# Batch 1's values and mix results take the path of later batches, batch 2's loads move, odd mixes move by 0.4 slots

## The chip, the cores and the metric

The kernel runs on one core of a Trainium2 chip. The metric is the device time of one execution in microseconds (us), lower is better; times before are the median of three runs. A profile is of one execution, and its span is a little shorter than that execution's time.

## What is computed

Eight batches of pooled attention, followed by a token mix and a channel MLP with affine scales and residuals. Keys and values are averaged over groups of 8 tokens, so 576 tokens give 72 pooled ones.

```python
# q, k, v: (8 batches, 8 heads, 576 tokens, 64)
k_p = k.reshape(B, H, 72, 8, D).mean(axis=3)
v_p = v.reshape(B, H, 72, 8, D).mean(axis=3)
attn = softmax(q @ k_p.T / 8)
x = (attn @ v_p) in the layout (B, 576, 512)
a1 = alpha1 * x + beta1
u = x + lam * einsum('ts,bsd->btd', w_tok, a1)
a2 = alpha2 * u + beta2
out = u + lam * (maximum(a2 @ w_ch1, 0) @ w_ch2)     # 512 -> 2048 -> 512
```

All inputs and the output are fp32; the matmuls take bf16 or fp16.

## The kernel before

The tokens of all batches are cut into 36 chunks of 128 rows. A batch has four chunks of 128 tokens and 64 tokens left over; the 64 of an even batch and of the odd one after it share a chunk. The list `chunks` puts them in this order: (0,0) to (0,3), (1,0) to (1,3), then (0,4), the shared one, then (2,0) and so on. Four chunks in this order make a block, of 512 rows, for the MLP: nine blocks, n = 0 to 8. Block 1 is exactly the four chunks (1,0) to (1,3); block 3 is (2,3), (3,0), (3,1), (3,2).

While TensorE works through the MLP of block n, the attention and token mix of batch n+1 are put between its matmuls. The order is written out by hand: for each block a list `todo` of pairs (slot, action) is filled and sorted by slot, and the actions are then issued in that order; every engine works through its own part of it strictly in order. A slot is about one group of four 512-wide matmuls. Slots 0 to 15 are `mlp_A(n, j)` (first MLP matmul, L604, ReLU on ScalarE, L609). Slots 16 to 31 are `mlp_B(n, m, part)` (second matmul, L638), four parts for each row group m; with the last part VectorE scales the sum by lam (L644), adds it to u (L645), and SP issues the store of the output (L647). Where slots are equal, what was put in the list first comes first. Batch 0 and the constants come before block 0, in a straight hand-written sequence.

One batch's attention has these steps:

- `load_k` (L91, SP) loads fp32 keys, two tiles of four heads; `sum_k` on POOL adds them pairwise (L160, L162); `att_K` pools on TensorE (L405, L411), and VectorE copies the result to `kp` (L417). With `behind` given, `load_k`, `load_v` and `load_rem` first write a tiny memset with that engine, so that the load is not issued before the engine's place in the order.
- The queries come in bf16 by a casting DMA from POOL (L77). `att_F` transposes them, with TensorE for batches 0 and 1 and by a transposing DMA from SP (L363) from batch 2 on. `cast_rem`, `att_Frem` and `rem_qT` do the same for the 64 remaining tokens.
- The values. Batches 0 and 1 load them in fp16 by a casting DMA from POOL (`load_v16`, L106 and L111), and `first_V` pools them with six matmuls for each half of the heads (L431, L433), with two copies by VectorE (L436). From batch 2 on `load_v` loads fp32 values by SP (L137), 72 partitions with 8 tokens each, one tile for each half of the heads, and `att_V` pools one pair of heads with three VectorE additions (L443 twice, L445). The tag `v_u` has two buffers for both kinds of tile.
- `att_S4` computes the scores of four heads (L475, L482) from `kp` and the queries, ScalarE the exponentials, `att_AV` the weighted values (L519, L523) and their division by the sums (L525, L527), `att_X` the scaled input `xs` of the mix (L534, L538).
- `mix_T(b, c)` is the token mix of chunk c (L567); VectorE adds the residual (L571) and writes a bf16 copy `u_bf` (L574; four buffers).
- `mix_uT` turns `u_bf` into columns of `u_fm`, the input of `mlp_A`. For batches 0 and 1 TensorE transposes (L588) and ScalarE copies (L590); for later batches and for the shared chunk (0,4) SP issues a transposing DMA (L583). One matmul of `mlp_A(n, 0)` reads the columns of all four chunks of its block.

SP's queue, in order, holds key, value and remainder loads, the transposing DMAs and the output stores; a store waits in it for VectorE's L645. POOL's queue holds the casting DMAs of queries and weights (`load_w1`, `load_w2`) between POOL's arithmetic.

The list of block 0 for batch 1 (`first`), as far as it matters: `att_K(1,0)` and `att_K(1,1)` at slots 6.4 and 9.4, `att_S4(1,0)` and `att_S4(1,1)` at 9.0 and 13.6, `bias_row(1)` on VectorE at 4.5, `first_V` at 11.0 and 12.2. The mixes of every batch are at 21.0 + 1.3c.

Of the kernel before, what the change touches and what calls it, by code (L numbers as in the profile page):

```python
# [23 lines left out]
def kernel(  # L24
# [18 lines left out]
    nc = tc.nc  # L43
# [27 lines left out]
    def rows(src, b, u):  # L71
        return src[b, 4 * u:4 * u + 4, 0:512, :].rearrange("h (p c) d -> p h (c d)", c=4)
# [13 lines left out]
    def load_k(b, u, behind=None):  # L86

        raw = work.tile([P, 4, 4, D], FP, tag="k_raw", bufs=2, name="k_raw")
        if behind is not None:
            behind.memset(raw[:, 0, 0, 0:1], 0.0)  # L90
        nc.sync.dma_start(out=raw.rearrange("p h c d -> p h (c d)"), in_=rows(k, b, u))  # L91
        st1[b]["raw"][u] = raw

    def load_v16(b, parts=(0, 1, 2)):

        if 0 in parts:
            t = work.tile([P, 6, H, D], F16, tag="v_u", bufs=2, name="v16")
            main, rest = t[:, 0:4].rearrange("p c h d -> p (c h d)"), t[0:32, 4:6]
            main = main.rearrange("p (h c d) -> p h c d", h=H, c=4)
            rest = rest.rearrange("p c h d -> p (c h d)").rearrange(  # L100
                "p (h c d) -> p h c d", h=H, c=2)
            st1[b]["v"] = main, rest
        main, rest = st1[b]["v"]
        for part in parts:
            if part == 1:
                nc.gpsimd.dma_start(  # L106
                    out=rest.rearrange("p h c d -> p h (c d)"),
                    in_=v[b, :, 512:576, :].rearrange("h (p c) d -> p h (c d)", c=2))
            else:
                u = part // 2  # L110
                nc.gpsimd.dma_start(  # L111
                    out=main[:, 4 * u:4 * u + 4].rearrange("p h c d -> p h (c d)"),
                    in_=rows(v, b, u))
# [188 lines left out]
    def setup_rowsum(tcx):  # L302

        trc = P if tcx < 4 else REM
        cols = slice(P * tcx, P * tcx + trc)
        ps = gp("ps_rs")
        for sc in range(5):
            nc.tensor.matmul(out=ps[:, 0:trc], lhsT=ones_bf if sc < 4 else ones_lo,
                             rhs=wtT[:, sc, cols], start=(sc == 0), stop=(sc == 4))
        nc.scalar.copy(out=wtT[64:65, 4, cols], in_=ps[64:65, 0:trc])  # L310
# [128 lines left out]
    def att_V(b, hp):  # L439

        t = st1[b]["v"][hp // 2][:, 2 * (hp % 2):2 * (hp % 2) + 2]
        for n in (4, 2):
            nc.vector.tensor_tensor(out=t[:, :, 0:n], in0=t[:, :, 0:n], in1=t[:, :, n:2 * n],  # L443
                                    op=ALU.add)
        nc.vector.tensor_tensor(out=vp1_pool[hp][:, :, 0:64], in0=t[:, :, 0], in1=t[:, :, 1],  # L445
                                op=ALU.add)
# [129 lines left out]
    def mix_uT(key):  # L576
        s = st2[key]
        i = where[key]
        blk, at = i // 4, i % 4
        if blk not in u_fm:  # L580
            u_fm[blk] = work.tile([P, 4, 512], BF, tag="u_fm", bufs=3, name="u_fm")
        if key[0] > 1 or key == (0, 4):
            nc.sync.dma_start_transpose(out=u_fm[blk][:, :, 128 * at:128 * at + 128],  # L583
                                        in_=s["u_bf"])
            return
        ps_uT = gp("ps_uT").bitcast(BF)
        for cc in range(4):
            nc.tensor.transpose(out=ps_uT[0:P, 128 * cc:128 * cc + 128],  # L588
                                in_=s["u_bf"][:, 128 * cc:128 * cc + 128], identity=identity_bf)
        nc.scalar.copy(out=u_fm[blk][:, :, 128 * at:128 * at + 128],  # L590
                       in_=ps_uT[:, 0:512].rearrange("p (c t) -> p c t", t=128))
# [115 lines left out]
    att_AV(0, 7)  # L707
    for u in range(2):
        load_k(1, u, nc.vector)
    setup_rowsum(0)  # L710
    setup_wtok(2, nc.scalar.copy)
    setup_rowsum(1)
# [2 lines left out]
    setup_rowsum(2)  # L715
    keep_warm(1)
    load_w1(3)
    load_v16(1, (0, 1))
    setup_rowsum(3)
    mix_T(0, 0, nc.gpsimd)  # L720
    mix_T(0, 1, nc.gpsimd)
    load_v16(1, (2,))
    for g in range(3):
        load_w2(g)
    setup_bias(0)
# [16 lines left out]
    def attention(b):  # L742


        first = b == 1
        todo = []
        if first:
            for hp in range(4):
                todo.append((2.6 + 0.9 * hp, lambda hp=hp: att_F(b, hp)))
            todo.append((3.5, lambda: cast_rem(b, nc.gpsimd)))  # L750
            todo.append((3.65, lambda: load_w2(3)))
            todo.append((7.4, lambda: att_Frem(b, nc.scalar.copy)))
        if b < B - 1:
            at = 27.0 if first else 10.0
            todo.append((at, lambda: att_F(b + 1, 0)))
            todo.append((at + 0.1, lambda: att_F(b + 1, 2)))
            at = 28.0 if first else 25.5
            todo.append((at - 1.0, lambda: cast_rem(b + 1, nc.gpsimd)))
            todo.append((at, lambda: att_Frem(b + 1)))
        for u in range(2):  # L760
            todo.append((3.6 + 0.1 * u if first else -0.9 + 1.2 * u,
                         lambda u=u: sum_k(b, u, nc.gpsimd)))
            todo.append((6.4 + 3.0 * u if first else 4.1 + 2.0 * u,
                         lambda u=u: att_K(b, u, nc.vector.tensor_copy)))
            if first:
                todo.append((11.0 + 1.2 * u, lambda u=u: first_V(b, u)))
        for u in range(2):
            at = (9.0 if first else 6.3, 13.6)[u]
            todo.append((at, lambda u=u: att_S4(b, u)))
            for k, dt in enumerate((0.1, 0.1, 0.1, 0.7, 1.7, 1.75) if u else (0.1, 0.1, 0.1, 1.1, 2.1, 3.1)):  # L770
                todo.append((at + dt, lambda u=u, k=k: st1[b]["exp", u](k)))
            for i, dt in enumerate((2.9, 3.4, 4.6, 5.1) if u else (5.7, 6.2, 2.9, 3.4)):
                h = 4 * u + i
                todo.append((at + dt, lambda h=h: att_AV(b, h)))
                if i % 2:
                    todo.append((at + dt + 0.1, lambda h=h: att_X(b, h - 1, h + 1)))
        if not first:
            for hp in range(4):
                todo.append((0.2 + 2.0 * hp, lambda hp=hp: att_V(b, hp)))
        for c in range(5):  # L780
            at = 21.0 + 1.3 * c
            if c < 4 or b % 2:
                todo.append((at, lambda c=c: mix_T(b, c)))
                key = (b, c) if c < 4 else (b - 1, 4)
                if first and c in (2, 3):
                    at += 1.3 * c - 2.0
                elif first and c < 2:
                    at += 1.0
                todo.append((at + 1.8, lambda key=key: mix_uT(key)))
        return todo  # L790

    for n in range(NBLK):
        todo = []
        for j in range(0 if n else 4, NJ):
            todo.append((j, lambda j=j: mlp_A(n, j)))
        for m in range(4):
            for part in range(4):
                at = 16 + 4 * m + part
                todo.append((at, lambda m=m, part=part: mlp_B(n, m, part)))
        if n == 0:  # L800
            todo.append((4.5, lambda: bias_row(1)))
            todo.append((6.2, lambda: setup_rowsum(4)))
            todo.append((8.3, setup_wtok_odd))
            for g in range(2, 4):
                todo.append((4 * g - 0.8, lambda g=g: setup_bias(g)))
        if n == NBLK - 1:
            for g in range(4):
                todo.append((2.0 + 3.0 * g, lambda g=g: scale_w2(g)))
        b = n + 1
        if b < B:  # L810
            todo += attention(b)
            if b + 1 < B:
                new_batch(b + 1)
                gate = nc.vector if b == 1 else None
                for u in range(2):
                    at = 21.0 + 0.2 * u
                    todo.append((at, lambda b=b, u=u: load_k(b + 1, u, gate)))
                    at = (21.0 if b == 1 else 0.4) + 0.1 * u
                    todo.append((at, lambda b=b, u=u: load_q_bf(b + 1, u)))
                    at = 19.0 + 0.2 * u if b == 1 else 3.5 + 4.0 * u  # L820
                    todo.append((at, lambda b=b, u=u: load_v(b + 1, u, behind=gate)))
                todo.append((20.9, lambda b=b: load_rem(b + 1, behind=gate)))
        for _, do in sorted(todo, key=lambda x: x[0]):
            do()

# [29 lines left out]
```

The softmax here doesn't subtract the row's maximum and nothing guards it: scores larger than these inputs give would overflow.

## Time and profile before

| what | us |
|---|---|
| median of 3 runs | 352.65 (352.64 to 353.04) |
| the profiled execution | 353.1 |
| its span | 351.1 |
| TensorE busy | 337.8 |
| VectorE busy | 226.0 |
| first MLP matmul of block 0 (L604) | at 30.51 |
| first MLP matmul of block 1 | at 74.69 |
| first MLP matmul of block 2 | at 110.41 |
| first MLP matmul of block 3 | at 147.26 |

The profile gives, for each engine, its busy time and the idle time before an instruction with what ended it. PE is TensorE, PEld its weight loads, DVE VectorE, ACT ScalarE, POOL GpSimd, SP SyncE; SPq is SP's queue of DMA issues. Line numbers are those of the kernel before. Times of single instructions are from the start of the span. In timelines the columns are start, duration, engine, line, operation, output and inputs, count, and in brackets the idle time before with its releaser. Sizes of DMA packets are those written.

### The profile page before, as it was taken

How to read it: one execution, taken by the hardware profiler on the slowest of the kernel's cores; microseconds unless marked ns; L12 is line 12 of the kernel's file. 1: busy time of each engine (PE TensorE's matmuls, PEld its weight loads, DVE VectorE, ACT ScalarE, POOL GpSimd, SP SyncE). 2: the span in 40 equal slices, each digit the busy share in tenths (PEclk: the TensorE clock that was granted, in tenths of full speed). 3: DMA queues.
4: the chain of work that ended last, by engine and by line, in shares of the span. 5: the costliest groups of instructions: out<-in, count | busy, mean ns of one | idle time of the engine just before them, and what ended most of it. 6: DMA issues, size and time to landing. Idle time of an engine off the chain costs nothing.

```text
span 351.1 us, 5881 instructions
## 1 busy us (share of the span) xinstructions
PE 337.8 (96%) x2206; PEld 178.8 (51%) x2247; DVE 226.0 (64%) x476; ACT 150.6 (43%) x283; POOL 78.9 (22%) x93
## 2 busy tenths in 40 slices
PE   7989999999999999999999999999999999999995
PEld 2667654455544554455445544554455445545544
DVE  6564048788696769775967697948785883037511
ACT  4564972238502850087008800791069105703800
POOL 8578600072017000710071005300510000000000
PEclk9999999999999999999999999999999999999999
DMA  8999980898738942897189719991820032011012
GB/s 129 196 213 241 217 151 0 188 248 174 134 113 203 216 63 66 231 190 121 55 224 189 127 52 211 186 146 51 228 75 1 32 90 77 0 60 62 0 54 66
DMA packets 66045, 44.57 MB, mean 127 GB/s; under 512 B 32409, under 2 KB 57309, under 8 KB 66018
## 3 DMA queue, kind: packets, MB, share of 16 engines
q1 hardware_dynamic: 50486, 33.18, 39.4%
q0 software_dynamic: 15072, 10.76, 21.1%
q8 instruction: 17, 0.28, 0.3%
q10 hardware_dynamic: 460, 0.27, 0.3%
q14 instruction: 10, 0.08, 0.1%
HBM read 38.30 MB, written 9.44 MB: 136 GB/s over the span
## 4 chain that ended last, share of the span: by engine, by line
PE 85%; DVE 8%; ACT 3%; issue 2%; POOL 1%; POOLq 0%; DVEq 0%; ACTq 0%
PE ps_h L604 33%; PE ps_ch L638 30%; PE ps_tok L567 12%; DVE x_tm L527 2%; PE ps_s L475 2%; PE ps_av L519 2%; DVE xs L534 2%; DVE v_u L443 1%; PE ps_ch L627 1%; ACT wtT L299 1%; PE ps_kp L405 1%; DVE rec L525 1%; PE ps_sc L455 1%; DVE ps_ch L644 1%; PE ps_v L431 1%
## 5 line engine op out<-in xcount | busy, mean ns | idle before, releaser
L609 ACT ACTIVATE Hj<-ps_h,bias_cols 128x512 bf16<-128x512 f32 x144 | 98.4, 689 | 150.7 <-PE ps_h L604 149.2
L604 PE MATMUL ps_h<-u_fm,w 128*128 128x512 bf16 (+1 forms) x571 | 132.2, 374 | 2.0 <-ACT Hj L609 0.5
L638 PE MATMUL ps_ch<-w,Hj 128*128 128x512 bf16 x543 | 128.7, 379 | 1.1 <-issue 0.6
L604 PEld LDWEIGHTS <-w 128*128 128x128 bf16 x592 | 63.9, 114 | 52.4 <-issue 4.0
L638 PEld LDWEIGHTS <-Hj 128*128 128x128 bf16 x560 | 52.8, 98 | 60.9 <-issue 1.6
L567 PE MATMUL ps_tok<-xs,wtT 128*128 128x512 bf16 (+3 forms) x200 | 44.8, 380 | 1.9 <-DVE xs L534 1.8
L644 DVE TENSOR_TENSOR ps_ch<-lam_bc,ps_ch 128x512 f32<-128x512 f32 x32 | 22.2, 693 | 33.2 <-PE ps_ch L638 33.0
L145 POOL CAST rem_q<-rem_raw 128x256 bf16<-128x256 f32 x7 | 3.3, 475 | 151.6 <-DMA rem_raw<-in_q_dram 151.6
L571 DVE TENSOR_TENSOR u_sb<-x_tm,ps_tok 128x512 f32<-128x512 f32 (+1 forms) x40 | 27.3, 683 | 11.3 <-PE ps_tok L567 11.2
L527 DVE TENSOR_TENSOR x_tm<-ps_av,rec 128x320 f32<-128x320 f32 x64 | 31.5, 492 | 2.3
L645 DVE TENSOR_TENSOR u_sb<-u_sb,ps_ch 128x512 f32<-128x512 f32 x35 | 24.0, 687 | 13.7 <-PE ps_ch L638 12.5
L504 ACT ACTIVATE ET<-ps_s 72x512 f16<-72x512 f32 x56 | 32.3, 591 | 0.0
L525 DVE RECIPROCAL rec<-ps_av 128x5 f32<-128x5 f32 x64 | 12.2, 190 | 30.2 <-PE ps_av L523 30.0
L567 PEld LDWEIGHTS <-wtT 128*128 128x128 bf16 (+3 forms) x200 | 16.9, 100 | 23.6 <-DVE xs L534 3.4
L443 DVE TENSOR_TENSOR v_u<-v_u 72x512 f32<-72x512 f32 (+1 forms) x48 | 27.3, 570 | 0.8
L574 DVE TENSOR_TENSOR u_bf<-u_sb,al_bc 128x512 bf16<-128x512 f32 x34 | 25.8, 758 | 2.5 <-DMA u_fm<-u_bf 1.4
L160 POOL TENSOR_TENSOR k_raw<-k_raw 128x512 f32<-128x512 f32 x14 | 19.1, 1367 | 13.1 <-DMA k_raw<-in_k_dram 12.6
L534 DVE TENSOR_TENSOR xs<-x_tm,lamal_bc 128x512 bf16<-128x512 f32 x29 | 20.1, 692 | 1.0
L519 PEld LDWEIGHTS <-ET 72*128 72x128 f16 x256 | 14.1, 97 | 8.9 <-issue 0.4
L162 POOL TENSOR_TENSOR k_bf<-k_raw 128x512 bf16<-128x512 f32 x14 | 17.8, 1275 | 1.1
L519 PE MATMUL ps_av<-vp,ET 72*128 72x66 f16 x256 | 15.8, 193 | 0.2 <-issue 0.2
L417 DVE CAST kp<-ps_kp 128x288 bf16<-128x288 f32 x14 | 6.4, 456 | 12.9 <-PE ps_kp L411 12.3
(119 smaller groups left out, 228.0 us busy)
## 6 DMA issues: line engine op xcount, KB each, us to landing
out_dram<-u_sb SPq DMA_DIRECT2D x32, 256.0 KB
k_raw<-in_k_dram SPq DMA_DIRECT2D x14, 512.0 KB
v_u<-in_v_dram SPq DMA_DIRECT2D x12, 512.0 KB
q_bf<-in_q_dram POOLq DMA_DIRECT2D x16, 256.0 KB, 6.6
w<-in_moe_w_ch_dram POOLq DMA_DIRECT2D x8, 512.0 KB, 14.6
v<-in_v_dram POOLq DMA_DIRECT2D x4, 256.0 KB, 9.8
rem_raw<-in_q_dram SPq DMA_DIRECT2D x15, 64.0 KB
rem_raw<-in_k_dram SPq DMA_DIRECT2D x15, 64.0 KB
```

The source lines that it names most:

```text
L443: nc.vector.tensor_tensor(out=t[:, :, 0:n], in0=t[:, :, 0:n], in1=t[:, :, n:2 * n], op=ALU.add)
L504: nc.scalar.activation(out=o, in_=i, func=AF.Exp, bias=0.0, scale=0.125)
L519: nc.tensor.matmul(out=av[:, odd + c, :], lhsT=ET[:, m0:m0 + 128], rhs=vp1[:, hh, :])
L527: nc.vector.tensor_tensor(out=x[:, 1 - odd:6 - odd, dd:dd + D], in0=av[:, :, 0:64], in1=rec.unsqueeze(2).to_broadcast((P, 5, D)), op=ALU.mult)
L534: eng.tensor_tensor(out=xs[:, 0:4, cols], in0=x[:, 1:5, cols], in1=lamal_bc[:, cols].unsqueeze(1).to_broadcast((P, 4, D * (h1 - h0))), op= ...
L567: nc.tensor.matmul(out=ps_tok[p0:p1], lhsT=wtT[0:kk, at, P * c:P * c + p1 - p0], rhs=xs_pool[i][0:kk, sc, :], start=(sc == 0), stop=(sc == 4))
L571: nc.vector.tensor_tensor(out=s["u"][p0:p1, :], in0=x[p0:p1, 1 + c if c < 4 else 5 - 5 * i, :], in1=ps_tok[p0:p1, 0:DM], op=ALU.add)
L574: eng.tensor_tensor(out=s["u_bf"], in0=s["u"], in1=al2_bc, op=ALU.mult)
L604: nc.tensor.matmul(out=ps_h[:, t0:t1], lhsT=w1_of(cc, j), rhs=u_fm[n][:, cc, t0:t1], start=(cc == 0), stop=(cc == 3))
L609: nc.scalar.activation(out=t, in_=ps_h, func=AF.Relu, bias=bias_cols[:, j:j + 1], scale=1.0)
L638: nc.tensor.matmul(out=ps, lhsT=Hj[n, j][:, 128 * m:128 * m + 128], rhs=w2[j // 4][:, j % 4, :], start=(j == 0), stop=(j == NJ - 1))
L644: nc.vector.tensor_tensor(out=ps, in0=lam_bc, in1=ps, op=ALU.mult)
```

## The change

Batch 1 no longer takes batch 0's path. Its values are loaded as fp32 by SP, right after its keys, and pooled by `att_V` on VectorE at slots 4.0, 5.5, 7.0 and 8.5 of block 0; the two `load_v16` of batch 1 on POOL and its two `first_V` go. Its mix results go through the transposing DMA at the mix's slot + 1.8, as in later batches. The loads of batch 2 in block 0 move: values from slot 19.0 to 13.0, remainders from 20.9 to 16.9, keys and queries from 21.0 to 17.0. The mixes of all odd batches move from 21.0 + 1.3c to 21.4 + 1.3c, and their transposes with them.

```diff
@@ mix_uT
-        if key[0] > 1 or key == (0, 4):
+        if key[0] or key[1] == 4:
             nc.sync.dma_start_transpose(out=u_fm[blk][:, :, 128 * at:128 * at + 128],
                                         in_=s["u_bf"])
             return
@@ the sequence ahead of block 0
     for u in range(2):
         load_k(1, u, nc.vector)
+    for u in range(2):
+        load_v(1, u, behind=nc.vector)
     setup_rowsum(0)
...
     load_w1(3)
-    load_v16(1, (0, 1))
     setup_rowsum(3)
     mix_T(0, 0, nc.gpsimd)
     mix_T(0, 1, nc.gpsimd)
-    load_v16(1, (2,))
     for g in range(3):
         load_w2(g)
@@ attention(b)
-            if first:
-                todo.append((11.0 + 1.2 * u, lambda u=u: first_V(b, u)))
...
-        if not first:
-            for hp in range(4):
-                todo.append((0.2 + 2.0 * hp, lambda hp=hp: att_V(b, hp)))
+        for hp in range(4):
+            at = 4.0 + 1.5 * hp if first else 0.2 + 2.0 * hp
+            todo.append((at, lambda hp=hp: att_V(b, hp)))
         for c in range(5):
-            at = 21.0 + 1.3 * c
+            at = 21.0 + 0.4 * (b % 2) + 1.3 * c
             if c < 4 or b % 2:
                 todo.append((at, lambda c=c: mix_T(b, c)))
                 key = (b, c) if c < 4 else (b - 1, 4)
-                if first and c in (2, 3):
-                    at += 1.3 * c - 2.0
-                elif first and c < 2:
-                    at += 1.0
                 todo.append((at + 1.8, lambda key=key: mix_uT(key)))
@@ the loop over blocks, loads of batch b + 1
-                    at = 21.0 + 0.2 * u
+                    at = (17.0 if b == 1 else 21.0) + 0.2 * u
                     todo.append((at, lambda b=b, u=u: load_k(b + 1, u, gate)))
-                    at = (21.0 if b == 1 else 0.4) + 0.1 * u
+                    at = (17.0 if b == 1 else 0.4) + 0.1 * u
                     todo.append((at, lambda b=b, u=u: load_q_bf(b + 1, u)))
-                    at = 19.0 + 0.2 * u if b == 1 else 3.5 + 4.0 * u
+                    at = 13.0 + 0.2 * u if b == 1 else 3.5 + 4.0 * u
                     todo.append((at, lambda b=b, u=u: load_v(b + 1, u, behind=gate)))
-                todo.append((20.9, lambda b=b: load_rem(b + 1, behind=gate)))
+                todo.append((16.9 if b == 1 else 20.9, lambda b=b: load_rem(b + 1, behind=gate)))
```

## The prediction

> **What bounds the kernel now.** I read the page first: share of each engine, then the chain that ended last.
>
> ```profile
> PE 337.8 (96%) x2206; PEld 178.8 (51%) x2247; DVE 226.0 (64%) x476; ACT 150.6 (43%) x283; POOL 78.9 (22%) x93
> PE 85%; DVE 8%; ACT 3%; issue 2%; POOL 1%; POOLq 0%; DVEq 0%; ACTq 0%
> ```
>
> PE is busy nearly all the time and carries 85% of the chain, so PE work removed anywhere is worth its own length, and any new wait of PE is paid in full. Next come the timelines of PE and DVE around block 0, where nearly all of the change lies.
>
> ```profile
> 42.44 0.30 PE L475 MATMUL ps_s<-qT,kp 64*72 64x256 bf16 x2
> ...
> 45.67 0.60 PE L431 MATMUL ps_v<-v,pool_v 128*72 128x256 f16 x4
> 46.20 0.40 PE L433 MATMUL ps_v<-v,pool_vr 32*72 32x256 f16 x2
> 46.53 0.70 PE L349 MATMUL ps_bias<-b2c_bf,w 128*128 128x1 bf16 x16
> ...
> 74.69 4.48 PE L604 MATMUL ps_h<-u_fm,w 128*128 128x512 bf16 x20
> ```
>
> ```profile
> 38.83 0.46 DVE L417 CAST kp<-ps_kp 128x288 bf16<-128x288 f32 x1 [7.37 <-PE ps_kp L411]
> ...
> 73.13 0.69 DVE L645 TENSOR_TENSOR u_sb<-u_sb,ps_ch 128x512 f32<-128x512 f32 x1
> ...
> 112.02 1.14 DVE L443 TENSOR_TENSOR v_u<-v_u 72x512 f32<-72x512 f32 x2
> 113.19 0.29 DVE L445 TENSOR_TENSOR vp<-v_u 72x128 f16<-72x128 f32 x1
> ```
>
> PE reaches the first scores of batch 1 (L475) at 42.44; the keys that they need were copied by DVE at 38.83, after an idle DVE. Block 1's first matmuls start at 74.69, with no gap. A head pair's pooling on DVE (L443 twice, L445) takes 1.14 + 0.29 us. The third view is the DMA queues, asked for short windows (packets, MB, share); here 26 to 28 us, 30 to 32, 40 to 42, and 72 to 74. Queue 0 holds what POOL issues, queue 1 what SP issues.
>
> ```profile
> q0 software_dynamic: 308, 0.29, 86.8%
> q1 hardware_dynamic: 298, 0.14, 35.3%
> ...
> q1 hardware_dynamic: 239, 0.24, 44.9%
> q0 software_dynamic: 239, 0.24, 71.1%
> ...
> q0 software_dynamic: 125, 0.44, 109.6%
> ...
> q1 hardware_dynamic: 713, 0.77, 107.2%
> ```
>
> Two things are to be seen. Where both queues have work they send equal numbers of packets, even where the packets differ in size (298 of 0.5 KB against 308 of 0.9 KB). And queue 0's packets after 38 us, the w2 loads, are large: 0.44 MB in 125, some of which are tiny, so 4 KB each. The fourth view, POOL and SP:
>
> ```profile
> 33.62 1.27 POOL L160 TENSOR_TENSOR k_raw<-k_raw 128x512 f32<-128x512 f32 x1 [1.20 <-DMA k_raw<-in_k_dram]
> 37.94 1.26 POOL L160 TENSOR_TENSOR k_raw<-k_raw 128x512 f32<-128x512 f32 x1 [1.18 <-DMA k_raw<-in_k_dram]
> ```
>
> ```profile
> 23.14 1.24 SPq L91 DMA_DIRECT2D k_raw<-in_k_dram x2
> ...
> 74.31 3.32 SPq L363 DMA_TRANSPOSE qT<-q_bf x2
> 77.72 1.20 SPq L381 DMA_TRANSPOSE rem_qT<-rem_q x1
> 78.97 1.26 SPq L583 DMA_TRANSPOSE u_fm<-u_bf x1
> ```
>
> Batch 1's two key tiles, issued at 23.14, land only at 33.6 and 37.9: the DMA engines are the scarce thing from 18 to 50 us (the third to sixth slice of their row on the page read 9, 9, 9 and 8). The v of batch 1 will be queued behind these keys.
>
> **What the Trainium skill says.** "DMA: Bandwidth & Descriptors", section Queues, rings and completion order: each DMA engine goes round robin over the queues that have work, and changes only at packet boundaries. The windows above agree (239 against 239). It follows that a queue with small packets gets a small share of the bytes beside one with large ones. The same page, Issuing engines are not separate DMA queues: loads from POOL and SP share the same 16 engines, so moving v from one queue to the other frees no bandwidth. "TensorE: Matmul & The Clock Gate", section What's actually happening: after an idle window of about 3.4 us the PE clock halves, and comes back after about as long a busy one. The trace has a cold start that fits: four L431 matmuls took 0.95 us at 11.27 and 0.60 us at 45.67.
>
> **The change part by part.**
>
> *Removed from PE.* Two poolings of v: 45.67 to 46.53 and 48.19 to 49.06, 1.73 us. Sixteen transposes of mix results (L588): each four push the next work back 0.22 us (64.51 to 64.73), 0.88 us. Together 2.6 us of PE, all on the path. ACT loses four copies of 0.59 us and DVE four of 0.24; neither bounds there.
>
> *v of batch 1 by SP, pooled by DVE.* In DVE's order the poolings of head pairs 0 and 1 now stand ahead of the first kp copy (L417), and those of pairs 2 and 3 ahead of the second. So a v that lands late holds the keys, and these hold PE. To cost nothing v's first half must land by 42.44 - 0.1 - 0.46 (copy) - 2 x 1.45 (poolings) - 0.67 (bias_row, between them) = 38.3 us. When does it land? On queue 0 w1's last packets go out near 33.6 (the 1 KB packets give way to v's smaller ones in the windows 32 to 34 and 34 to 36). There queue 1 still has about 380 key packets of 1 KB to send (it sent 299 in 34 to 36 and 19 after; plus 0.4 us of the 306 in 32 to 34). So far v's packets of 0.25 to 0.5 KB stood beside them, and the keys had landed by 37.9. With v gone from queue 0, the 512 packets of w2 stand there at once: 4 KB at 0.21 MB/us (42 to 44: 0.40 MB), 0.0195 us each, against 0.0027 for a key packet (0.77 MB in 2 us at 72 to 74). A pair takes 0.022 us, 45 pairs per us, so 380 take 8.4 us: the keys end at 42.0. The remaining 132 w2 packets pair with v's 2 KB packets, of which each half has 288 (72 partitions x 4 heads) at some 0.0093 us (0.93 MB from 64 to 68): 3.8 us, 45.8. The other 156 go alone, 1.5 us, 47.3, and 0.6 to the landing: 47.9. DVE then needs 4.0 us up to the copied keys; PE goes on at 51.95, 9.5 us late. It loses 9.0 net, since waits of PE on ACT of 0.46 and a little more just behind (43.94) are overtaken. The price of a large packet beside a small one isn't in this trace, so bounds: if the queues shared bytes instead of packets, queue 1 would move 0.11 MB/us, v's first half would land at 43.2 and the stall be 4.9; with no overlap at all inside a pair it is 10.3. I take 9.0 because packet counts matched in every window in which both queues were full. The second half lands near 51, while DVE still does the first; the second kp copy is done by 55, before PE comes to it.
>
> *Clock.* After over 9 us of idle I charge the slow clock over one window, 3.4 us at half speed, less what is latency there: 1.5 us (bounds 0 and 2.5).
>
> *Mix results by DMA.* The SP order is now: output of row group 1, three transposes, output of group 2, a qT transpose of batch 2, the transpose of chunk (1,3), the other qT. Block 1's first matmul reads all four chunks at once. Count from the first mix at 59.55. With mixes 2 and 3 one slot (0.86) later and transposes gone, PE is ready for block 1 at 73.9 (74.69 less 0.88, rounded). The output of group 2 waits for DVE's L645, before at 73.13 to 73.8, now about 73.2, as its mix of chunk (0,4) comes 0.6 earlier. Then 0.4 for the output's issue, 1.7 for qT, and about 2.4 from the transpose's issue to landing (the window of 78.97 to 81.4 for the one before). It lands at 77.7: PE stalls 3.8 us. Bounds: 2 if qT doesn't delay it, 5.5 with a loaded queue.
>
> *Third batch's loads sooner.* They go behind nothing that is late: before, keys landed by 73.7 and PE waited 0.17 us for them (81.41). Gain 0. Their seven memsets (0.06 to 0.1 us) lie mostly in DVE idle; two fall into its busy run ahead of the first mix: 0.2 us lost.
>
> *Odd mixes 0.4 later.* In the instruction order only mixes 2 and 3 step behind one more group of four matmuls; the first, whose wait for xs is the visible one (0.63 at 59.55, 0.40 at 133.0), doesn't move. Gain 0. In block 2 the transpose of (3,2) moves behind rem_qT and lands near 147.6 against 147.26: up to 0.4 lost. I take 0.1.
>
> Sum: 9.0 + 1.5 + 3.8 + 0.2 + 0.1 - 2.6 = +12.0 us. The profiled span of 351.1 becomes 363.1. That execution took 353.1, 0.45 above the median of 352.65; on the median it gives 364.6.
>
> **The rivals.**
> *Shares by bytes:* v's first half at 43.2, stall 4.9 (4.4 net) and about 1 of clock: 4.4 + 1 + 3.8 + 0.3 - 2.6 = +6.9, 359.5. For it: the sizes of 4 KB against 1 KB were never met in the trace. Against: 0.5 KB against 0.9 KB shared by count.
> *The transposes are hidden:* SP gets (1,3) away early enough; only the first stall stays, 364.6 - 3.8 = 360.8. Against: SP is in order and out waits for L645.
> *Worse:* the second idle of 3.8 us also halves the clock, or the loads of batch 2 still fill queue 1 when the transposes are issued: +2 to +5, 367 to 370.
> *Faster:* queue 1 gets through ahead of w2, keys by 34.7 and v by 38.1, just under the 38.3 that decides; DVE has idle for its 5.8 us of pooling there. If the transpose of (1,3) lands within PE's last row group too, the 2.6 us stay: 350.0. For it: DVE's idle of 7.37 us. Against: equal packet counts. With the second stall alone left it would be 353.9, still slower.
>
> **How the numbers follow.** Both stalls near these sizes, 361.5 to 368: 0.60. Bytes shared or one stall much smaller, 354 to 361.5: 0.24. Worse than 368: 0.10. Faster: 0.05, and 0.01 lies within 0.2% (0.7 us, about what a measurement of this kernel can tell from none). The range 358.5 to 369 leaves out about 2 in 10. Slower has 0.60 + 0.24 + 0.10 = 0.94.
>
> **What would show it.** In the changed profile: an idle of PE ahead of L475 of about 9 us, ended by DVE kp; DVE ahead of the first L443 waiting for the DMA of v_u until about 48; the second key sum of POOL at 42 to 43 instead of 37.94; equal packet counts in both queues from 34 to 42, with 4 KB on one side; a gap of PE of about 4 us ahead of block 1, ended by the DMA u_fm<-u_bf. I am wrong if v lands before 39 us, or if block 1 starts without a gap.

## The result, and the profile after

| what | before | after |
|---|---|---|
| median, us | 352.64 (352.59 to 353.04, 4 runs) | 369.83 (366.69 to 372.6, 4 runs) |
| the profiled execution, us | 353.1 | 366.69 |
| its span, us | 351.1 | 365.0 |
| first matmul of block 0, us | 30.51 | 29.85 |
| first matmul of block 1 | 74.69 | 87.05 |
| first matmul of block 2 | 110.41 | 124.08 |
| first matmul of block 3 | 147.26 | 161.09 |

The changed kernel takes 1.0455 times as long as before, 95% interval 1.0388 to 1.0522. (The ratio leaves out the longest execution, of 372.6 us, so it is a little below that of the medians.) It also scatters: the other three took 366.69, 369.29 and 370.37 us at mean granted clocks of 0.981, 0.975 and 0.972. Nearly the whole loss lies in block 0, which grew from 44.18 to 57.20 us; from block 2 on the two kernels run alike to 0.2 us.

The page of the changed kernel: busy shares, the row of granted clock (tenths, forty slices of the span), and the chain that ended last by engine.

```profile
PE 337.8 (93%) x2179; PEld 176.6 (48%) x2219; DVE 229.8 (63%) x488; ACT 148.2 (41%) x279; POOL 76.4 (21%) x90
PEclk9999959998999999999999999999999999999999
PE 78%; DVE 9%; DMA 7%; issue 2%; ACT 2%; POOL 1%; SPq 0%; POOLq 0%; DVEq 0%; ACTq 0%
```

TensorE has fewer instructions than before and yet the same 337.8 us of busy time: what was taken out was given back in matmuls that ran slowly. DMA, not on the chain's list before, now has 7% of it. The clock row has a 5 in the sixth slice (45.6 to 54.8 us) and an 8 in the tenth (82 to 91 us), which are the two places where PE stood still. The timeline of PE of the changed kernel shows them in the brackets, where the idle time ahead stands:

```profile
51.08 0.75 PE L316 MATMUL ps_wo<-identity_bf,wt_bf 128*128 128x128 bf16 x5 [10.56 <-DVE kp L417]
...
53.59 0.43 PE L475 MATMUL ps_s<-qT,kp 64*72 64x256 bf16 x2
...
87.05 6.17 PE L604 MATMUL ps_h<-u_fm,w 128*128 128x512 bf16 x20 [3.79 <-DMA u_fm<-u_bf]
```

The first wait, 10.56 us, ends with the copy of the pooled keys, the second, 3.79, with a transposing DMA. The 20 matmuls behind the second took 6.17 us, where before the same 20 took 4.48. The timelines of DVE and of POOL of the same kernel say why the keys were late:

```profile
47.22 1.14 DVE L443 TENSOR_TENSOR v_u<-v_u 72x512 f32<-72x512 f32 x2 [16.75 <-DMA v_u<-in_v_dram]
...
50.58 0.45 DVE L417 CAST kp<-ps_kp 128x288 bf16<-128x288 f32 x1
...
81.75 0.69 DVE L645 TENSOR_TENSOR u_sb<-u_sb,ps_ch 128x512 f32<-128x512 f32 x1
```

```profile
33.17 1.27 POOL L160 TENSOR_TENSOR k_raw<-k_raw 128x512 f32<-128x512 f32 x1 [2.11 <-PE ps_h L604]
...
40.87 1.25 POOL L160 TENSOR_TENSOR k_raw<-k_raw 128x512 f32<-128x512 f32 x1 [4.56 <-DMA k_raw<-in_k_dram]
```

DVE stood for 16.75 us in front of the first pooling of v, waiting for its load, with the copy of keys that were ready since 38 (PE pooled them at 37.82) queued behind it. The second key tile came at 40.87 instead of 37.94. The DMA queues of the changed kernel from 36 to 38 us (packets, MB, share):

```profile
q0 software_dynamic: 104, 0.35, 86.8%
q1 hardware_dynamic: 102, 0.14, 21.9%
```

Equal counts again, with 3.4 KB to a packet on POOL's queue (w2) and 1.4 KB on SP's (keys and v); from 40 to 42 it was 87 against 88. And SP's queue of the changed kernel ahead of block 1:

```profile
82.47 0.35 SPq L647 DMA_DIRECT2D out_dram<-u_sb  x1
82.92 1.30 SPq L363 DMA_TRANSPOSE qT<-q_bf  x1
84.28 1.25 SPq L583 DMA_TRANSPOSE u_fm<-u_bf  x1
```

The last transpose that block 1 needs (L583, chunk (1,3)) was issued at 84.28, behind a store that waited for DVE's L645 (81.75 to 82.44) and behind a transpose of batch 2's queries; PE went on at 87.05, so it landed just before that. Last, the stretches of the changed kernel around both stalls (length, busy us of PE, PEld, DVE, ACT and POOL, granted clock, DMA share, GB/s):

```profile
30.00:60.00 30.00, 18.97 (x183) 12.74 (x184) 9.48 (x22) 16.11 (x32) 8.12 (x8) 0.83 0.82 169
60.00:100.00 40.00, 35.35 (x213) 17.05 (x214) 28.01 (x63) 12.35 (x25) 8.29 (x8) 0.96 0.70 150
```

The 13.9 us between the spans add up as follows. First stall: 10.56, less a wait of 0.46 on ACT (at 43.94) that it swallowed, +10.1. Second stall +3.79. PE work taken out, put at the 2.61 that was worked out ahead. What is left of block 0's growth, 57.20 - (44.18 + 10.1 + 3.79 - 2.61) = +1.74, I put down to the slow clock behind the first stall. The trace shows about 1.2 of it directly: from L316 at 51.08 to the L604 at 54.72 PE took 3.64 us, at a granted clock of 0.57, and before it took 2.94 from L316 (41.00) to the same L604 (43.94), of which 0.46 was the wait on ACT. The other 0.6 is only what is left of the sum. Block 1 took 37.03 where it took 35.33 to 35.34 in the runs without a stall ahead of it and with batch 2's loads moved: +1.70 of slow clock. Those 35.34 are themselves 0.38 less than the 35.72 of before. Block 2 +0.16, the start of block 0 -0.66 (in all runs it lay between 29.85 and 32.03, in no order with the edits); what is left is below the 0.1 to which the spans are given.

### The profile page after: what moved, and what is told of

Read it like the earlier page. It is cut to its first block, busy times and chain, and to the rows that moved or that the text cites. A ratio compares the mean times of both kernels' runs of the same rounds, so it can differ in the third digit from the quotient of the medians.

```text
span 365.0 us, 5842 instructions
## 1 busy us (share of the span) xinstructions
PE 337.8 (93%) x2179; PEld 176.6 (48%) x2219; DVE 229.8 (63%) x488; ACT 148.2 (41%) x279; POOL 76.4 (21%) x90
## 4 chain that ended last, share of the span: by engine, by line
PE 78%; DVE 9%; DMA 7%; issue 2%; ACT 2%; POOL 1%; SPq 0%; POOLq 0%; DVEq 0%; ACTq 0%
PE ps_h L604 32%; PE ps_ch L638 26%; PE ps_tok L567 10%; DMA v_u<-in_v_dram 6%; PE ps_s L475 2%; DVE x_tm L527 2%; DVE xs L534 2%; PE ps_av L519 2%; PE ps_ch L627 1%; PE ps_kp L405 1%; DVE rec L525 1%; ACT wtT L299 1%; DMA u_fm<-u_bf 1%; DVE v_u L443 1%; DVE ps_ch L644 1%
## 5 line engine op out<-in xcount | busy, mean ns | idle before, releaser
L604 PE MATMUL ps_h<-u_fm,w 128*128 128x512 bf16 (+1 forms) x572 | 134.8, 379 | 5.3 <-DMA u_fm<-u_bf 3.8
L604 PEld LDWEIGHTS <-w 128*128 128x128 bf16 x592 | 64.1, 115 | 57.8 <-issue 9.7
L443 DVE TENSOR_TENSOR v_u<-v_u 72x512 f32<-72x512 f32 (+1 forms) x56 | 30.8, 550 | 17.7 <-DMA v_u<-in_v_dram 16.7
L645 DVE TENSOR_TENSOR u_sb<-u_sb,ps_ch 128x512 f32<-128x512 f32 x35 | 24.0, 687 | 13.6 <-PE ps_ch L638 12.5
L574 DVE TENSOR_TENSOR u_bf<-u_sb,al_bc 128x512 bf16<-128x512 f32 x34 | 26.5, 779 | 3.3 <-DMA u_fm<-u_bf 2.2
L567 PEld LDWEIGHTS <-wtT 128*128 128x128 bf16 (+3 forms) x200 | 16.9, 100 | 24.0 <-DVE xs L534 3.4
L162 POOL TENSOR_TENSOR k_bf<-k_raw 128x512 bf16<-128x512 f32 x14 | 18.8, 1339 | 1.1
L77 POOL DMA_DIRECT2D q_bf<-in_q_dram x16 | 12.4, 781 | 0.8 <-POOLq L833 0.8
```

The costliest lines, as they stand in the source:

```text
L567: nc.tensor.matmul(out=ps_tok[p0:p1], lhsT=wtT[0:kk, at, P * c:P * c + p1 - p0], rhs=xs_pool[i][0:kk, sc, :], start=(sc == 0), stop=(sc == 4))
L574: eng.tensor_tensor(out=s["u_bf"], in0=s["u"], in1=al2_bc, op=ALU.mult)
L604: nc.tensor.matmul(out=ps_h[:, t0:t1], lhsT=w1_of(cc, j), rhs=u_fm[n][:, cc, t0:t1], start=(cc == 0), stop=(cc == 3))
```

## The experiments

Theories, as put to the test. *Packets:* w2's 4 KB packets on POOL's queue slow SP's small ones one to one, v is late, and DVE's order passes this on to the keys. *Bytes:* the queues share bytes, and v is late because SP has more to carry. *SP's order:* the second stall is the place of one transpose in SP's queue, not the transposing DMA as such. Ratios are against the kernel before on the same chip; the kernels of the experiments ran on three chips, so ratios are compared and not times. Line numbers are those of the changed kernel unless said.

**Batch 1's values back on their old path.** From the changed kernel: `load_v` and `att_V` of batch 1 out, `load_v16` and `first_V` in.

```diff
-    for u in range(2):
-        load_v(1, u, behind=nc.vector)
+    load_v16(1, (0, 1))
...
+    load_v16(1, (2,))
...
+        if first:
+            for u in range(2):
+                todo.append((11.0 + 1.2 * u, lambda u=u: first_V(b, u)))
```

> The changed kernel with batch 1's values loaded by POOL and pooled on TensorE as before; its mix results still go by transposing DMA. If v's late landing is the first stall: the idle of PE ahead of L316 (10.6 us) goes, the one ahead of block 1 (3.8 us) stays, with a slow clock behind it. 352.65 - 0.9 (transposes off PE) + 3.8 + about 2 of clock = 357.5 (356 to 359). If instead the earlier loads of batch 2 or the order of SP made the first stall, it stays above 366.

Measured: 357.57 us (357.22 to 358.46), ratio 1.0132 [1.0112, 1.0152]; L316 ran at 40.35 without a wait, block 0 took 47.38 us, and the wait ahead of block 1 was still there, 3.91 us. The values' path carries the first stall and nothing of the second: 1.0455 to 1.0132, about 11 us.

**Batch 1's mix results back on TensorE.** The complement: the old condition and the old offsets.

```diff
-        if key[0] or key[1] == 4:
+        if key[0] > 1 or key == (0, 4):
...
+                if first and c in (2, 3):
+                    at += 1.3 * c - 2.0
+                elif first and c < 2:
+                    at += 1.0
```

> The changed kernel with batch 1's mix results transposed on TensorE at their old distance; v still in fp32 by SP. If the transposing DMA of chunk (1,3) behind the store and qT is the second stall: no idle ahead of block 1, so 369.8 - 3.8 - about 2 of clock + 0.9 = 365 (363 to 366.5). If the gap ahead of block 1 has another cause (SP or DVE late from the first stall), it stays at 369 to 371.

Measured: 363.92 us (362.9 to 364.09), ratio 1.0302 [1.0281, 1.0322]. Block 1 started without a gap and took 35.33 us. The first stall was there, on PE's timeline of this kernel:

```profile
51.99 0.75 PE L316 MATMUL ps_wo<-identity_bf,wt_bf 128*128 128x128 bf16 x5 [11.38 <-DVE kp L417]
```

So without the second idle block 1 is 1.70 us shorter than in the changed kernel, although its own work is the same. That is the slow clock's price after 3.8 us of idle: the first 20 matmuls alone are 6.17 - 4.48 = 1.69 us longer there.

**w2 sent later.** All four groups of w2 go to POOL's queue at slot 3.75, behind POOL's key sums.

```diff
-    for g in range(3):
-        load_w2(g)
...
-            todo.append((3.65, lambda: load_w2(3)))
+            for g in range(4):
+                todo.append((3.75 + 0.01 * g, lambda g=g: load_w2(g)))
```

> The changed kernel with the four w2 loads issued by POOL behind both key sums instead of ahead of them; same bytes, later. Shares by packets: keys land near 35.5, v's first half near 38.5, PE idles at most 1 us there; the second stall stays: 352.65 - 2.6 + 3.8 + about 2 = 356 (354.5 to 359). If the loads of w1, keys and v by themselves fill the DMA engines (lack of bandwidth, whatever the order), v's first half lands after 43 and the time stays above 361.

Measured: 359.86 us (357.98 to 361.4), ratio 1.019 [1.0134, 1.0246]; a little above what was expected, as is the wait at L316 (at most 1 us was expected there); the four executions fall into two pairs, near 358.2 and 361.4 at granted clocks of about 0.995 and 0.985, and the trace is of one of the first pair. SP's queue had the engines to itself from 34 to 36 us (370 packets, 0.53 MB, 100% against 45 packets of POOL's). DVE's and PE's timelines of this kernel:

```profile
39.39 1.15 DVE L443 TENSOR_TENSOR v_u<-v_u 72x512 f32<-72x512 f32 x2 [9.07 <-DMA v_u<-in_v_dram]
```

```profile
43.25 0.52 PE L316 MATMUL ps_wo<-identity_bf,wt_bf 128*128 128x128 bf16 x5 [2.54 <-DVE kp L417]
```

With w2 out of the way v lands at 39.4 instead of 47.2 and the stall shrinks from 10.56 to 2.54 us; the one ahead of block 1 stays, 4.05. The first doesn't go: even an early v is not there for an instruction that stands ahead of the keys. This says that w2 is the cause, but not yet whether by its bytes or by its packets.

**w2 in small packets, where it was.** The same bytes in the same place; the tiles of w2 get 8 unused columns, so that a row of 1 KB is one packet. (This adds a line ahead, so lines here are one higher.)

```diff
-    w2 = [const.tile([P, 4, DM], BF, tag=f"w2_{g}", name=f"w2_{g}") for g in range(4)]
+    w2 = [const.tile([P, 4, DM + 8], BF, tag=f"w2_{g}", name=f"w2_{g}")[:, :, 0:DM]
+          for g in range(4)]
```

> The changed kernel with the rows of w2 in SBUF 8 elements apart, so that w2 arrives in 1 KB packets, four times as many; same bytes, same order of issue. Shares by packets: 118 pairs per us instead of 46, keys land at 37.5, v's first half near 41.5, PE idles about 5 instead of 10.6 us: 363 (361 to 366). Shares by bytes or plain lack of bandwidth: v lands near 46.5 as it does now and the time stays at 368 to 371.

Measured: 364.04 us (361.79 to 365.1), ratio 1.029 [1.0248, 1.0332], where *packets* had it. The queues of this kernel from 36 to 38 us, and its DVE:

```profile
q0 software_dynamic: 210, 0.22, 63.0%
q1 hardware_dynamic: 211, 0.33, 52.9%
```

```profile
42.46 1.14 DVE L444 TENSOR_TENSOR v_u<-v_u 72x512 f32<-72x512 f32 x2 [10.73 <-DMA v_u<-in_v_dram]
```

Counts are equal once more, 210 to 211, but now twice as many in 2 us, and SP's queue carries 0.33 MB instead of 0.14. v lands 4.8 us sooner, though block 0 began 1.5 us later in this execution, and PE's wait at L316 is 4.29 instead of 10.56. If bytes were shared, cutting the packets could not have moved them from one queue to the other. *Bytes* is out for these loads.

**The pooling of v behind both key copies.** DVE's order alone; the loads stay late.

```diff
-            at = 4.0 + 1.5 * hp if first else 0.2 + 2.0 * hp
+            at = (9.5, 9.45, 9.55, 9.6)[hp] if first else 0.2 + 2.0 * hp
```

> The changed kernel with the poolings of v put behind both kp copies in DVE's order (slots 9.45 to 9.6, head pair 1 first); all DMA as it is. v still lands near 47, but holds only the weighted values, not the keys: PE's idle of 10.6 us ahead of L316 goes, one of 2 to 4 comes ahead of the first L519 of batch 1. 360 (358 to 363). If PE waits for v directly as long as it waited for the keys, time stays above 366.

Measured: 363.19 us (362.6 to 363.81), ratio 1.0272 [1.0234, 1.031], at the upper edge of what was expected. L316 ran at 40.40 and L475 at 41.84, both without a wait. PE then waited in two other places of this kernel:

```profile
44.65 0.29 PE L405 MATMUL ps_kp<-pool_main,k_bf 128*128 128x64 bf16 x4 [2.03 <-POOL k_bf L162]
...
50.87 0.38 PE L519 MATMUL ps_av<-vp,ET 72*128 72x66 f16 x4 [3.63 <-DVE vp L445]
```

The first is the late second key tile, the second the late v itself, met where it is used. So of the 10.56 us about 5 came from DVE's order and 5.7 from the late loads: both edits of the values' path, its queue and its place, have a share.

**The transpose of chunk (1,3) sooner.** By 0.2 slots.

```diff
-                todo.append((at + 1.8, lambda key=key: mix_uT(key)))
+                todo.append((at + (1.6 if first and c == 3 else 1.8), lambda key=key: mix_uT(key)))
```

> The changed kernel with one number altered: the transposing DMA of chunk (1,3) 0.2 slots sooner, so that it stands ahead of the store of row group 2 and of qT in SP's queue. If that place in the queue is the second stall: the transpose lands before PE ends block 0, no idle ahead of block 1, 369.8 - 3.8 - 2 = 364 (362.5 to 366). If the transposing DMA itself is too slow for the distance, a gap of over 2 us stays: above 367.

Measured: 365.68 us (363.17 to 367.41), ratio 1.0337 [1.0288, 1.0386]. The time lies where the first case had it, but not for its reason: the gap ahead of block 1 fell from 3.79 to 2.33 us and did not go, although the transpose now stands ahead of the store. Block 1 behind this shorter gap took 35.34 us, with no slow clock. The first stall in this profile was 11.94 us, so the ratio is no clean measure of the second.

What the remaining 2.33 us wait for is not settled. The profile puts their end down to a pooling of batch 2 on DVE (L443), with which these matmuls share no tile. All four transposes had left SP by 83.12; the queues of this kernel from 83 to 84 us:

```profile
q0 software_dynamic: 380, 0.19, 142.7%
q1 hardware_dynamic: 1, 0.00, 0.2%
```

POOL's queue was loading batch 2's queries, issued at 80.06 (L77), and SP's, with the transposes in it, all but stood; it sent 515 packets from 84 to 85, and 526 from 86 to 87, when the query loads ended. So in time the transposes stood behind these loads, which the change had also moved forward, from slot 21 to 17. No run moved them alone beside the transposes, so this is a rival left open.

**Odd mixes back in their old slots.** The other way to bring that transpose forward: at slot 26.7 instead of 27.1, ahead of the part at slot 27 with its store.

```diff
-            at = 21.0 + 0.4 * (b % 2) + 1.3 * c
+            at = 21.0 + 1.3 * c
```

> The changed kernel with the odd mixes at their old slots, all else changed. The transpose of (1,3) is then due at 26.7, ahead of the store of row group 2 at 27: if the 0.4 slots are what put it behind, the idle ahead of block 1 shrinks to under 1.5 us and the time is 364 to 366.5. If the 0.4 slots don't matter to it, the idle stays at 3.8 and the time at 368 or more.

Measured: 363.81 us (363.43 to 364.23), ratio 1.0274 [1.0232, 1.0316], a touch below what was expected. SP's queue and PE of this kernel:

```profile
77.16 4.03 SPq L583 DMA_TRANSPOSE u_fm<-u_bf  x3
84.29 0.34 SPq L647 DMA_DIRECT2D out_dram<-u_sb  x1
84.73 2.64 SPq L363 DMA_TRANSPOSE qT<-q_bf  x2
```

```profile
85.70 4.48 PE L604 MATMUL ps_h<-u_fm,w 128*128 128x512 bf16 x20 [0.62 <-DMA u_fm<-u_bf]
```

All transposes of block 1 now leave SP ahead of the store. The gap is 0.62 us, the 20 matmuls take 4.48 again, block 1 takes 35.34. So 3.2 us of the second stall, and the slow clock behind it, came from the 0.4 slots. The 0.62 us that stay need not be the transposing DMA's own: here too POOL's query loads ran beside the last transposes (540 packets against 490 from 82 to 84 us). (The first stall was still there, 9.47 us.)

**PE kept busy through both stalls.** Matmuls into an unused sum fill the waits (44 ahead of L316, 15 ahead of block 1); they add nothing to the output.

```diff
+            todo.append((8.25, lambda: keep_warm(44)))
...
+        if n == 1:
+            todo.append((-0.95, lambda: keep_warm(15)))
```

> The changed kernel with matmuls on a constant tile put into both stalls (44 ahead of L316, 15 ahead of block 1, 0.21 us each; they leave the output alone). If the clock that PE loses by idling is worth what is left over the two waits: granted clock back at 0.995 or more, 364 (363 to 365.5), and the runs within 1 us instead of 6. If the spread and the rest come from the DMA's own timing, time stays at 367 to 372 and scatters as before.

Measured: 365.64 us (364.77 to 367.43), ratio 1.0348 [1.0305, 1.039], just above what was expected. PE of this kernel, in the first stall:

```profile
41.63 9.66 PE L558 MATMUL ps_warm<-warm 128*128 128x512 bf16 x44
...
53.28 0.52 PE L316 MATMUL ps_wo<-identity_bf,wt_bf 128*128 128x128 bf16 x5 [1.98 <-DVE kp L417]
```

The wait is as long as it was (41.6 to 53.3), but the mean granted clock is 0.995 and block 1 takes 35.34. The executions lie within 2.7 us, where those of the changed kernel lay within 5.9; within 1 was expected. Against the changed kernel's ratio it is about 1%, some 3.8 us, for the clock alone; as the intervals just touch, this size is rough.

**The two small parts alone.** The kernel before, with only batch 2's loads sooner and the odd mixes later. From the changed kernel:

```diff
-        if key[0] or key[1] == 4:
+        if key[0] > 1 or key == (0, 4):
...
-    for u in range(2):
-        load_v(1, u, behind=nc.vector)
+    load_v16(1, (0, 1))
...
+    load_v16(1, (2,))
...
+                todo.append((11.0 + 1.2 * u, lambda u=u: first_V(b, u)))
...
+                if first and c in (2, 3):
+                    at += 1.3 * c - 2.0
+                elif first and c < 2:
+                    at += 1.0
```

> The kernel before with only the two small parts of the change: batch 2's loads sooner and the odd mixes 0.4 slots later; batch 1 keeps its old path. From the other runs' blocks: block 1 0.4 us shorter through the loads, block 2 0.2 to 0.5 longer through the mixes: within 0.7 us of the kernel before. If the small parts have a share in the loss, over 1 us slower.

Measured: 353.87 us (352.24 to 355.62), ratio 1.000 [0.9973, 1.0028], as expected. Block 1 gained 0.38 us, block 2 lost 0.33. By themselves these edits are nothing, to within the interval's 1 us; the 0.4 slots cost only together with the transposing DMA.

**Three remedies together.** w2 later, v behind the keys, the transpose sooner.

```diff
+                todo.append((3.75 + 0.01 * g, lambda g=g: load_w2(g)))
...
+            at = (9.5, 9.45, 9.55, 9.6)[hp] if first else 0.2 + 2.0 * hp
...
+                todo.append((at + (1.6 if first and c == 3 else 1.8), lambda key=key: mix_uT(key)))
```

> The changed kernel with three repairs: w2 loads behind the key sums, poolings of v behind the kp copies, transpose of (1,3) ahead of the store. With no stall left and 2.6 us of PE removed: 350.2 (349.5 to 351.5), below the kernel before. If the DVE work or the transposes of the new path cost time of their own, 353 or more.

Measured: 352.94 us (351.62 to 358.43), ratio 0.9988 [0.9971, 1.0005]: a miss. Both stalls were gone and block 0 took 43.10 us, but PE waited 1.45 us for the mix's input in this kernel:

```profile
59.42 1.24 PE L567 MATMUL ps_tok<-xs,wtT 128*128 128x512 bf16 x5 [1.45 <-DVE xs L534]
```

All four poolings, 5.8 us, now stood together at 43.97 to 49.6 us, right ahead of DVE's busy run; before, that wait was 0.63. And PE waited 0.76 us in block 1 for `rem_qT`, whose transpose stood behind the store and both transposes of queries in SP's queue (issued at 77.10).

**The poolings split between the key copies.** w2 later; pairs 0 and 1 behind the first key copy, 2 and 3 behind the second; odd mixes in their old slots; the transpose of batch 2's remainders ahead of the queries'.

```diff
+                todo.append((3.75 + 0.01 * g, lambda g=g: load_w2(g)))
...
-            at = 28.0 if first else 25.5
+            at = 26.95 if first else 25.5
...
-            at = 4.0 + 1.5 * hp if first else 0.2 + 2.0 * hp
+            at = (6.5, 6.55, 9.45, 9.5)[hp] if first else 0.2 + 2.0 * hp
...
-            at = 21.0 + 0.4 * (b % 2) + 1.3 * c
+            at = 21.0 + 1.3 * c
```

> A repaired version: w2 loads behind the key sums, poolings of head pairs 0 and 1 behind the first kp copy and of 2 and 3 behind the second, odd mixes at their old slots, the transpose of batch 2's remainders ahead of the store of row group 2. If nothing but place and packets was wrong, the 2.6 us taken off PE and 0.4 of block 1 remain: 3 us below the kernel before on the same chip, 349.5 to 351. If the poolings on DVE or the transposing DMA crowd the mixes of batch 1 however they are placed, it ends within 1 us of the kernel before.

Measured: 350.64 us (349.6 to 353.42), ratio 0.9915 [0.9879, 0.9951], as expected. The interval lies below 1, so this is faster than the kernel before, if by less than 1%. DVE of this kernel:

```profile
38.72 0.46 DVE L417 CAST kp<-ps_kp 128x288 bf16<-128x288 f32 x1 [7.47 <-PE ps_kp L411]
40.19 1.14 DVE L443 TENSOR_TENSOR v_u<-v_u 72x512 f32<-72x512 f32 x2 [1.01 <-DMA v_u<-in_v_dram]
...
43.43 0.46 DVE L417 CAST kp<-ps_kp 128x288 bf16<-128x288 f32 x1 [0.40 <-PE ps_kp L411]
```

DVE waits for v for 1.01 us, in its idle time, and the keys stand ahead of it. Block 1 starts at 72.21 with no gap. Block 0 took 41.81 us, 2.37 less than before (against 2.61 of PE work taken out), and block 1 35.34, 0.38 less.

## Why the prediction held, and where it was off

The direction held, and so did both stalls and the two chains behind them: large packets that make v late and a v that holds the keys, and a transpose behind a store. The size was off: 364.6 was forecast, 369.83 measured, just above the range's end of 369 (the ratio of 1.0455 on the forecast's own 352.65 is 368.7, just inside). In the profiled execution the span grew by 13.9 instead of 12.0 us, the median by 17.2; the other executions took longer, at lower granted clocks. Step by step:

- *Removed from PE, 2.6.* Held as far as it can be seen: block 0 gave 2.37 where no stall covered it (the last run).
- *v lands at 47.9.* It was pooled from 47.22, and the keys were copied at 51.03 instead of 51.85. In part this closeness is luck: the second key tile came at 40.87 instead of 42.0, and v took 6.35 us behind it instead of 5.9. (Not all 512 packets of w2 stood there at 33.6, as the forecast has it: the last group was issued at 35.73, behind the others, which leaves the sum as it is.) Packets pair one to one at 4 KB too: 104 against 102 in the profile, and the run with w2 in small packets. This agrees with the Trainium skill, "DMA: Bandwidth & Descriptors", section Queues, rings and completion order: the engines take turns between queues packet by packet. The rival that shared bytes, with 359.5, is refuted.
- *PE stops at L475, 9.0 net.* This step was wrong in its place. PE stopped at L316, before it got there: the profile names the copy of `kp` (L417) as what released it, and in every run L316 either ran after that copy or, where the copy was early, did not wait. Why it needs it was not tested. `setup_wtok_odd` takes its PSUM tile from the one ring of six that `ps_kp` comes from too, so a buffer used again is likely; but `ps_wo` is only the fifth tile asked for after `ps_kp`, so a plain turn of six would not give it that one. Keys that came a little sooner than forecast thus cost more, 10.1 net, since the work of L316 and a group of L604 was not done during the wait (1.44 us of it in the kernel before, 41.00 to 42.44).
- *Clock, 1.5.* The term that was most undersized. After the first stall it cost about the forecast, 1.2 seen in the trace and at most 1.74; a like price, 1.70, fell due again after 3.79 us of idle, which I had only in a rival at 0.10. In 30 to 60 us the granted clock was 0.83. This fits the Trainium skill's "TensorE: Matmul & The Clock Gate", section What's actually happening, which has the clock halved after an idle window of about 3.4 us: 3.79 us of idle cost 1.70, 2.33 us (the run with the transpose sooner) nothing. How much of the other executions' further time is clock was not profiled; their times rise as their clock falls, and the run with PE kept busy gave about 1% back in the ratio.
- *Mix results by DMA, 3.8; odd mixes later, gain 0.* The stall was 3.79 and ended as described: store, query transpose, then the transpose of (1,3). (Two of its terms were off by as much in opposite directions: 1.36 us for the query transpose instead of 1.7, and 2.8 to PE's start instead of 2.4.) But the cause was booked in the wrong place. At the old slots the same path leaves 0.62 us; the 0.4 slots put (1,3) at 27.1, behind the store due at 27. What was counted as free was the bulk of the second stall.
- *Third batch's loads sooner, gain 0; memsets, 0.2 lost; block 2, 0.1 lost.* Block 1 gained 0.38, block 2 lost 0.16 here, 0.2 to 0.6 in other runs with the odd mixes later, and nothing in the two runs with them in their old slots; a loss to the memsets was not seen.
- *The rivals.* The transposes were not hidden (3.79), the faster case did not come (v at 47.22 against the 38.3 that decides). Half of the "worse" case came, the second slow clock, and the median lies in its 367 to 370. That batch 2's loads stand ahead of the transposes was not tried by itself; in the run with the transpose sooner it was POOL's query loads that ran while SP's queue stood.

## What to carry to other kernels

An instruction that waits for a load holds everything behind it on its in-order engine, so put it behind what is ready sooner: here about 5 of the 10.56 us went with the order alone, and all of it in the last run, where w2 came later too. When a load moves to another queue, look at the packet sizes on the queue that it will share engines with; here the queue with the smaller ones moved 0.14 MB beside 0.35, and the remedy is to send the large ones later or in smaller rows. And a step that is moved by a fraction of a slot is to be checked against every in-order queue that it issues to, since 0.4 slots put a transpose behind a store and cost 3 us and a slow clock.

## What the runs showed of the hardware

- While both queues had loads waiting, they kept equal packet counts whatever the sizes: 104 to 102 with 3.4 KB against 1.4, 210 to 211 after w2 had been cut to 1 KB. Beside transposing DMAs this did not hold: 380 to 1 from 83 to 84 us in the run with the transpose sooner. Why is open.
- An idle of 3.79 us of PE was followed by 20 matmuls in 6.17 us instead of 4.48, one of 3.63 us (the run with v behind the keys) by four in 1.90 instead of 1.05; one of 2.54, 2.33 or 0.62 us was followed by no slower ones in the profiled executions.
- DVE's sum and bf16 write of the mix result (L574) took 0.69 us in block 0 of the kernel before (62 to 68 us), while POOL was idle, and 0.86 to 1.38 in some stretches of the changed kernel and of the run with the transpose sooner (72 to 80 us), where POOL was summing keys or issuing loads of queries; POOL's own L162 took 1.60 there instead of 1.27. That they share something is a guess; no run took them apart.
